# Three edits to a one-core spectral-filter and mixture-of-experts kernel: when lists are cast, in which order the last units run, which maxima are re-read first

## The chip, the cores and the metric

The kernel runs on one core of a Trainium2 chip. The metric is the device time of one execution in microseconds (us); lower is better. Engine names are those of the profile: PE is TensorE (PEld its weight loads), DVE is VectorE, ACT is ScalarE, POOL is GpSimd, SP is SyncE, which here only issues DMAs.

## The reference

```python
X = np.fft.rfft(x, axis=1)                       # x: 8 batches x 2496 rows x 256
y = np.fft.irfft(X * (filt_r + 1j*filt_i)[None], n=2496, axis=1)
x = y.reshape(8*2496, 256)
noisy = x @ w_gate + np.log1p(np.exp(x @ w_noise)) * noise      # 8 experts
top2 = two largest of each row; top2_w = softmax over those two
for each expert e:                                # w1[e]: 256x1024, w2[e]: 1024x256
    out[rows that chose e] += top2_w * (np.maximum(x[rows] @ w1[e], 0) @ w2[e])
```

## The kernel before, in words

**Two streams.** `fft_stream` filters the eight batches (the transform is written as matmuls), writes the filtered rows with their gate weights to a DRAM tensor `y`, and routes each batch: per expert, a list of row numbers in the DRAM tensor `lst`, and a small table `tabi` that says which stretch of which expert's list is the s-th block. `expert` works through blocks of rows that share an expert. `run` interleaves the two by a pace table; a scheduler of the framework then orders each engine's instructions by its own estimate, so that an edit in one place moves instructions nearly everywhere behind it.

**A block.** `read_list` issues, on SP, the load of a block's row numbers into the tile `lt` (line 1100), and POOL casts them to integers, `ids` (line 1106). `gather` fetches 128 rows at a time from `y` by an indirect DMA that POOL issues (line 1156) into slots of one staging tile `stage` (four slots for gathered rows, named "xg", handed out in turn by `slot`). `flip` lets SP transpose them by DMA, `turn` splits them into a high and a low part (`mxh`, `mxl`), and `expert` multiplies: `hps` is the first layer in PSUM, ACT and DVE turn it into `hh` and `hl` (lines 1369, 1370), `yps` is the second layer, ACT scales it by the gate into one of four output slots of `stage` (line 1396), and POOL issues an indirect DMA that adds the slot's rows to `out` (line 1397). These scatters to `out` wait for each other from unit to unit, because two experts may hold the same row; those of one unit do not.

**Order of the blocks.** First the blocks that can be taken after each batch, in `parts`; after the last batch seven single blocks of 512 rows (`SINGLE`), then what is left of each expert's list in units: 14 of 256 rows, then 4 of 128 rows (`ENDS`; the table's other slots are taken only in a branch at the end that these inputs do not enter). In each phase but `SINGLE`, the list of the next block is read, and cast, before the present block is handed on. A unit of either size loads both weight matrices of its expert, in two 16-bit planes each, by `load_planes`.

**Maxima.** From the fifth batch on the expert layers run on scaled 16-bit pairs. The scales come from maxima: `ymax` of the filtered rows, by `xscale`, and `wmax` of the weights, by `wscales`, a generator that is stepped now and then. `wscales` first loads all 64 quarter matrices of weights (line 595, 256 KB each) and lets ACT square them and sum each row (line 599). From each half of the sums `powers` makes a power of two on DVE and PE, kept in `wtab`. Then `wscales` re-reads the filtered rows of the first two batches from `y` in 12 loads (line 610) and lets DVE take their maxima (line 615), since those batches' own pass takes none. What is still left of it is run through at once when the first scaled block is gathered. POOL copies the scale of a block's expert from `wtab` to `sc` (line 1147); `w1h` and `w1l` (lines 1201, 1202) need `sc`, and `mxh` and `mxl` need `xs`, the result of `xscale`.

Of the kernel before, what the change touches and what calls it, by code (L numbers as in the profile page):

```python
# [14 lines left out]
I32 = mybir.dt.int32  # L15
# [13 lines left out]
E, F = 8, 1024  # L29
# [22 lines left out]
ENDS = (UNIT, USUAL, NUNIT), (UNIT // 2, E // 2, E)  # L52
SW = 32
# [97 lines left out]
class Moe:  # L151
# [427 lines left out]
    def xscale(self, bt):  # L579

        nc = self.nc
        nc.vector.tensor_reduce(self.xm, self.ymax[:, :2 * bt + 2], axis=AX.XY, op=ALU.max)
        q = yield from self.powers(self.xm, 1, TX)
        t = self.xs[bt + 1] = self.cp.tile([128, 2], F32, name=f"xs{bt}")
        nc.vector.tensor_copy(t, q[:, :, 0])
        yield

    def wscales(self):
# [50 lines left out]

        yield from pairs(load, top, 8 * E)  # L640
# [8 lines left out]
        yield from pairs(load_y, top_y, len(Y))  # L649
# [441 lines left out]
    def read_list(self, i, s, size):  # L1091
# [13 lines left out]
        ids = self.P.tile([128, n, nt], I32, name="ids", bufs=6)  # L1105
        nc.gpsimd.tensor_copy(ids, t)
        return ids, n, nt, s, self.tabs[i]
# [28 lines left out]
    def gather(self, blk, i):  # L1136
# [12 lines left out]
        if self.tail(tabi):  # L1149
            w = self.wodd = (self.wodd + 1) % 3  # L1150
            if nt < BLK // 128:
                w = self.load_planes(tabi, s, w)
        xg = []
# [252 lines left out]
    def run(self):  # L1406
# [15 lines left out]
        def parts():  # L1422

            def cut(blk, ready):
                for i in range(blk[1]):
                    yield (*blk, ready), i

            for i in range(NB):
# [5 lines left out]
                it = (self.read_list(i, s, m * BLK) for s in range(a, b))  # L1434

                nxt = next(it)
                while nxt is not None:
                    blk, nxt = nxt, next(it, None)
                    for p in cut(blk, i + 1):
                        state["left"] -= 1  # L1440
                        yield p
            state["left"] = 1
            for s in range(SINGLE):
                yield from cut(self.read_list(NB, s, BLK), NB)
            self.more = [self.nc.values_load(self.tabs[NB + 1 + i][0:1, 0, n:n + 1], min_val=0, max_val=E * CAPB * BLK // u)  # L1445
                         for i, (u, n, _) in enumerate(ENDS)]
            it = (self.read_list(NB + 1 + i, s, u) for i, (u, n, _) in enumerate(ENDS) for s in range(n))
            soon = [next(it)]
            while soon:
                soon += [b for b in (next(it, None),) if b]  # L1450
                yield from cut(soon.pop(0), NB)
# [69 lines left out]
```

## Time and profile before

| what | value |
|---|---|
| median of 3 runs | 2194.17 us (2190.20 to 2196.07) |
| profiled execution, its own time | 2191.23 us |
| its span, first to last instruction | 2189.4 us |
| busy: PE, PEld | 2107.5 us (96%), 1596.5 us (73%) |
| busy: DVE, ACT, POOL | 1473.3 us (67%), 1286.4 us (59%), 1024.6 us (47%) |
| granted PE clock over the span | 0.99 of full speed |

The profile is of one execution. Its own time lies 1.8 us above its span and 2.9 us below the median of the runs, within their spread. PE is busy nearly all the time, so a change can save only where PE is idle or its clock is not fully granted.

### The profile page before, as it was taken

To read this page: it belongs to the slowest core of one execution; us is meant where nothing else is said; L and a number is where in the kernel's file an instruction comes from. 1 tells how busy PE (TensorE), PEld (TensorE's weight loads), DVE (VectorE), ACT (ScalarE), POOL (GpSimd) and SP (SyncE) were. 2 spreads that over 40 slices of the span, in tenths; PEclk is the share of its full clock that TensorE was granted. 3 is DMA by queue.
4 is the path that set the end of the run, shared out by engine and by line. 5 is a ranking of instruction groups with operands and counts; after the bars stand their busy time and mean duration, and the time that the engine had idled before them with its cause. 6 is when DMAs were issued, how large, how long until landed. Compare 5 with 4: busy or idle time off the path is not lost. (4 is left out here: it accounts for less than half of the span.)

```text
span 2189.4 us, 42880 instructions
## 1 busy us (share of the span) xinstructions
PE 2107.5 (96%) x14517; PEld 1596.5 (73%) x14517; DVE 1473.3 (67%) x3245; ACT 1286.4 (59%) x2505; POOL 1024.6 (47%) x946
## 2 busy tenths in 40 slices
PE   8779999999999999899999999999999999999996
PEld 6437888888888888666666666766666666667886
DVE  4866678767986787778766886579666664333443
ACT  6666774777567746665665556555566564333443
POOL 4133424533443343545544453544566555654653
PEclk9989999999999999999999999999999999999999
DMA  9688987999888866967766666856899999768996
GB/s 241 173 247 203 230 222 171 222 234 228 203 213 230 189 144 152 202 160 174 156 155 151 136 146 149 198 118 131 198 246 238 230 238 211 200 148 221 277 273 170
DMA packets 511675, 428.49 MB, mean 196 GB/s; under 512 B 215680, under 2 KB 397016, under 8 KB 511448
## 3 DMA queue, kind: packets, MB, share of 16 engines
q1 hardware_dynamic: 450135, 341.27, 59.2%
q0 software_dynamic: 61312, 84.40, 22.5%
q8 instruction: 116, 1.90, 0.4%
q14 instruction: 112, 0.91, 0.1%
HBM read 263.92 MB, written 122.03 MB: 176 GB/s over the span
## 5 line engine op out<-in xcount | busy, mean ns | idle before, releaser
L1397 POOL DMA_INDIRECT out<-stage,ids x316 | 527.3, 1669 | 339.8 <-ACT stage L1396 245.9
L1370 DVE SCALAR_TENSOR_TENSOR hl<-hps,hh 128x512 f16<-128x512 f32 (+3 forms) x712 | 432.2, 624 | 339.5 <-ACT hh L1369 279.1
L1156 POOL DMA_INDIRECT stage<-y,ids x316 | 348.4, 1103 | 538.2 <-DMA xt<-stage 425.5
L124 PE MATMUL yps<-w,hh 128*128 128x256 f16 (+1 forms) x2048 | 558.8, 279 | 9.0 <-ACT hh L1369 3.8
L125 PE MATMUL yps<-w,hh 128*128 128x256 f16 (+1 forms) x2048 | 553.2, 277 | 0.0
L126 PE MATMUL yps<-w,hl 128*128 128x256 f16 (+1 forms) x2048 | 543.4, 278 | 6.8 <-DVE hl L1370 6.5
L1369 ACT ACTIVATE hh<-hps 128x512 f16<-128x512 f32 (+3 forms) x712 | 375.6, 550 | 185.7 <-PE hps L126 161.6
L125 PE MATMUL hps<-mxl,w1h 128*128 128x512 f16 (+1 forms) x1024 | 394.3, 386 | 0.7 <-DVE mxl L1244 0.7
L126 PE MATMUL hps<-mxh,w1l 128*128 128x512 f16 (+1 forms) x1024 | 393.0, 385 | 0.0
L124 PE MATMUL hps<-mxh,w1h 128*128 128x512 f16 (+1 forms) x1024 | 385.5, 388 | 2.7 <-DVE hl L1370 1.7
L1396 ACT ACTIVATE stage<-yps,gt 128x256 f32<-128x256 f32 x316 | 143.2, 475 | 342.3 <-PE yps L126 169.8
L124 PEld LDWEIGHTS <-hh 128*128 128x128 f16 x1760 | 172.3, 98 | 51.3 <-ACT hh L1369 4.1
L126 PEld LDWEIGHTS <-hl 128*128 128x128 f16 x1760 | 171.5, 98 | 48.9 <-issue 3.0
L125 PEld LDWEIGHTS <-hh 128*128 128x128 f16 x1760 | 172.2, 98 | 38.1 <-issue 6.0
L126 PEld LDWEIGHTS yps<-w,hl 128*128 128x128 f32 x768 | 145.9, 192 | 15.8 <-DVE hl L1370 8.2
L124 PEld LDWEIGHTS yps<-w,hh 128*128 128x128 f32 x768 | 147.0, 192 | 12.5 <-ACT hh L1369 4.9
L125 PEld LDWEIGHTS yps<-w,hh 128*128 128x128 f32 x768 | 146.6, 192 | 4.4 <-issue 0.6
L542 ACT COPY yt<-q 117x1024 uint16<-117x1024 uint16 x96 | 90.8, 946 | 42.4 <-PE q L536 23.6
L126 PEld LDWEIGHTS <-w1l 128*128 128x128 f16 x640 | 62.6, 98 | 71.8 <-issue 1.1
L1226 DVE COPY stage<-xt 128x1024 uint16<-128x1024 uint16 (+2 forms) x174 | 109.8, 685 | 3.0 <-issue 1.9
L125 PEld LDWEIGHTS <-w1h 128*128 128x128 f16 x640 | 62.6, 98 | 54.0 <-issue 4.0
L124 PEld LDWEIGHTS <-w1h 128*128 128x128 f16 x640 | 62.6, 98 | 53.0 <-issue 6.2
(287 smaller groups left out, 4041.7 us busy)
## 6 DMA issues: line engine op xcount, KB each, us to landing
stage<-w SPq DMA_DIRECT2D x328, 256.0 KB
x<-x SPq DMA_DIRECT2D x88, 256.0 KB
fd<-c SPq DMA_DIRECT2D x77, 240.0 KB
fi<-wpl SPq DMA_DIRECT2D x18, 1024.0 KB
fx<-fd SPq DMA_DIRECT2D x140, 128.0 KB
out<-z SPq DMA_DIRECT2D x24, 702.0 KB
wp<-w SPq DMA_DIRECT2D x64, 256.0 KB
fr<-w SPq DMA_DIRECT2D x16, 1024.0 KB
```

The lines of the kernel that those rows point to most:

```text
L124: nc.tensor.matmul(o, lh, rh, start=start, stop=False)
L125: nc.tensor.matmul(o, lh, rl, start=False, stop=False)
L126: nc.tensor.matmul(o, ll, rh, start=False, stop=stop)
L542: e = nc.scalar.copy(yt.bitcast(U16)[:, :k, :256].rearrange("p g (two d) -> p g two d", two=2), p.bitcast(U16)[:RP, :2 * m].rearrange("p ( ...
L1156: self.pin(lambda: nc.gpsimd.indirect_dma_start(out=x.bitcast(I32), out_offset=None, in_=self.y[:BLK + ready * ROWS], in_offset=bass.Indir ...
L1226: nc.vector.tensor_copy(xu.rearrange("p (t two) -> p two t", two=2), ent[3][0][:, 2 * kc:2 * kc + 2, :w])
L1369: hold(lambda: nc.scalar.activation(h, p, AF.Relu))
L1370: v = hold(lambda: nc.vector.scalar_tensor_tensor(l, p, 0.0, hf[0], op0=ALU.max, op1=ALU.subtract))
L1396: nc.scalar.activation(o, p, AF.Copy, scale=gate[:, t])
L1397: a = nc.gpsimd.indirect_dma_start(out=self.io["out"][:BLK + ready * ROWS], out_offset=bass.IndirectOffsetOnAxis(ap=ids[:, t:t + 1], axis= ...
```

## The change

Three edits. (1) `read_list` can return the cast as a function: the list's load is issued where it was, and POOL's cast is issued when the block begins. `SINGLE` and the units read one and two lists ahead. (2) The 4 units of 128 rows stand among the 14 of 256 (`MIXED`: after the 5th, 8th, 11th and 14th of them), so that the last two units are one of 256 and one of 128; `gather` skips slots until a unit's first slot is a multiple of its size. (3) `wscales` re-reads the filtered rows of the first batches before the weights instead of after them; `xscale` asserts that this is done.

```diff
+MIXED = sorted(((i, s) for i, (_, n, _) in enumerate(ENDS) for s in range(n)), key=lambda u: u[1] * 3 + 4 if u[0] else u[1])
...
     def xscale(self, bt):
...
+        assert self.seen
...
     def wscales(self):
...
+        yield from pairs(load_y, top_y, len(Y))
+        self.seen = True
         yield from pairs(load, top, 8 * E)
         for a, t in enumerate((TW1, TW2)):
             q = yield from self.powers(self.wmax[:, a * E:a * E + E], E, t, True)
...
-        yield from pairs(load_y, top_y, len(Y))
         self.scaled = True
...
-    def read_list(self, i, s, size):
+    def read_list(self, i, s, size, late=False):
...
-        ids = self.P.tile([128, n, nt], I32, name="ids", bufs=6)
-        nc.gpsimd.tensor_copy(ids, t)
-        return ids, n, nt, s, self.tabs[i]
+
+        def cast():
+            ids = self.P.tile([128, n, nt], I32, name="ids", bufs=6)
+            nc.gpsimd.tensor_copy(ids, t)
+            return ids, n, nt, s, self.tabs[i]
+
+        return cast if late else cast()
...
     def gather(self, blk, i):
...
+        while (self.turns.get("xg", -1) + 1) % nt:
+            self.slot("xg")
...
     def run(self):
...
-                it = (self.read_list(i, s, m * BLK) for s in range(a, b))
+                it = (self.read_list(i, s, m * BLK, True) for s in range(a, b))
...
-                    for p in cut(blk, i + 1):
+                    for p in cut(blk(), i + 1):
...
-            for s in range(SINGLE):
-                yield from cut(self.read_list(NB, s, BLK), NB)
-            self.more = [...]
-            it = (self.read_list(NB + 1 + i, s, u) for i, (u, n, _) in enumerate(ENDS) for s in range(n))
+            it = (self.read_list(NB, s, BLK, True) for s in range(SINGLE))
             soon = [next(it)]
             while soon:
                 soon += [b for b in (next(it, None),) if b]
-                yield from cut(soon.pop(0), NB)
+                yield from cut(soon.pop(0)(), NB)
+            self.more = [...]
+            it = (self.read_list(NB + 1 + i, s, ENDS[i][0], True) for i, s in MIXED)
+            soon = [next(it), next(it)]
+            while soon:
+                soon += [b for b in (next(it, None),) if b]
+                yield from cut(soon.pop(0)(), NB)
```

How the instructions stand now, at three places. Lines of the changed kernel are 1 to 9 above those of before (L617 is L615, L560 is L559, L577 is L576, L1406 is L1397).

DVE, where `wscales` begins, in the second batch's first blocks, before:

```order
L398 TENSOR_TENSOR tl<-fx,th 128x512
L340 TENSOR_TENSOR xl<-x,xh 117x512
L1079 TENSOR_TENSOR ro<-ro,rx 56x128
L1244 TENSOR_TENSOR mxl_2214<-xps,mxh_2213 128x512
L340 TENSOR_TENSOR xl<-x,xh 117x512
L426 TENSOR_TENSOR a<-q_1865,fr 128x512
```

And with the change:

```order
L341 TENSOR_TENSOR xl<-x,xh 117x512
L1082 TENSOR_TENSOR ro<-ro,rx 56x128
L1253 TENSOR_TENSOR mxl_2213<-xps,mxh_2212 128x512
L617 TENSOR_REDUCE ymax<-wp 117x1
L341 TENSOR_TENSOR xl<-x,xh 117x512
L427 TENSOR_TENSOR a<-q_1865,fr 128x512
L428 TENSOR_TENSOR b<-b,fi 128x512
L399 TENSOR_TENSOR tl<-fx,th 128x512
L617 TENSOR_REDUCE ymax<-wp 117x1
```

The 12 maxima of the re-read rows (`ymax<-wp`) moved here, among the next 95 rows of DVE.

PE, ahead of the first scaled block (`xm` is what `powers` transposes and multiplies, `pd` its powers of two), before:

```order
L126 MATMUL yps<-w_11225,hl 128x256
L446 MATMUL q_10083<-cf,a 128x2x64 x4
L576 MATMUL xm<-pd,small 128x1 x2
L457 MATMUL u_11105<-G,wg 32x360 x4
L343 MATMUL q_11129<-xh,hl 120x512
L344 MATMUL q_11129<-xh,hl 120x512
L345 MATMUL q_11129<-xl,hl 120x512
```

And with the change:

```order
L125 MATMUL yps<-w_11223,hh 128x256
L577 MATMUL xm<-pd,small 128x8 x2
L560 MATMUL xm<-ident,wmax 8x128
L126 MATMUL yps<-w_11223,hh 128x256
L127 MATMUL yps<-w_11223,hl 128x256
L577 MATMUL xm<-pd,small 128x8
L458 MATMUL u_11103<-G,wg 32x360 x4
L344 MATMUL q_11127<-xh,hl 120x512
L345 MATMUL q_11127<-xh,hl 120x512
L346 MATMUL q_11127<-xl,hl 120x512
L577 MATMUL xm<-pd,small 128x8
```

Before, only the scale of the filtered rows (`128x1`) stood this late; now both scales of the weights (`128x8`) do, the second with two matmuls between its transpose and its product.

POOL, the end of the units, before (numbers tell the units' lists apart):

```order
L1397 DMA out<-stage_84,ids_28198 21104x256
L1178 ISA
L1178 COPY gt_28958<-stage_84 128x1
L1180 TENSOR_SCALAR gt_28958<-gt_28958,sc_28942,xs7_20026 128x1
L1397 DMA out<-stage_84,ids_28392 21104x256
L1397 DMA out<-stage_84,ids_28584 21104x256
L1397 DMA out<-stage_84,ids_28778 21104x256
```

And with the change:

```order
L1187 ISA
L1187 COPY gt_28906<-stage_84 128x1
L1189 TENSOR_SCALAR gt_28906<-gt_28906,sc_28890,xs7_20024 128x1
L1406 DMA out<-stage_84,ids_28537 21104x256 x2
L1406 DMA out<-stage_84,ids_28696 21104x256 x2
L1406 DMA out<-stage_84,ids_28879 21104x256
```

Four scatters of four units, each behind the one before, ended the kernel; now the last are two of a unit of 256 rows, which need not wait for each other, and one of 128.

## Rows read from the trace of the kernel before

**Rows 1.** Busy time by stretch: us, engines (instructions), PEclk, DMA share, GB/s.

```profile
0.00:187.00 187.00, 153.60 (x817) 98.77 (x818) 123.54 (x383) 119.05 (x212) 52.23 (x54) 0.94 0.76 215
187.00:870.00 683.00, 666.64 (x4294) 583.02 (x4293) 521.77 (x1138) 461.28 (x932) 282.30 (x230) 1.00 0.86 204
870.00:905.00 35.00, 27.11 (x171) 20.51 (x169) 26.62 (x45) 18.36 (x35) 20.40 (x20) 0.95 1.11 206
905.00:1540.00 635.00, 630.57 (x4419) 431.86 (x4418) 475.63 (x1073) 377.83 (x692) 307.65 (x277) 1.00 0.69 154
1540.00:2175.00 635.00, 629.63 (x4824) 462.34 (x4822) 325.78 (x609) 309.93 (x636) 358.91 (x365) 1.00 0.93 226
2175.00:2189.40 14.40, 0.00 (x0) 0.00 (x0) 0.00 (x0) 0.00 (x0) 3.12 (x2) 0.62 0.18 22
```

**Rows 2.** Waits of PE, 830 to 905 us: total us, times, longest.

```profile
PE yps L126 <- DVE hl L1370: 4.2, 2, 3.4
PE q L446 <- DVE a L428: 1.3, 1, 1.3
PE u L457 <- ACT G L447: 0.8, 1, 0.8
```

**Rows 3.** Timeline of DVE, 868 to 898 us: start, us, instruction [idle before <-releaser].

```profile
875.36 0.95 DVE L615 TENSOR_REDUCE ymax<-wp 117x1 f32<-117x768 bf16 x1 [1.86 <-DMA wp<-y]
...
896.50 0.15 DVE L585 COPY xs<-xm 128x2 f32<-128x2 f32 x1
```

**Rows 4.** Lines 615 and 599: duration ns min/median/max, first and last start, forms.

```profile
L615 DVE TENSOR_REDUCE ymax<-wp x12: 929/1204/1221, 839.2 to 890.0; 117x1 f32<-117x1024 bf16 x8, 117x1 f32<-117x768 bf16 x4
...
L599 ACT ACTIVATE wp<-wp x64: 621/632/708, 187.4 to 734.8; 128x512 f32<-128x512 f32 x64
```

**Rows 5.** Timeline of POOL, the last scatters.

```profile
2169.94 1.59 POOL L1397 DMA_INDIRECT out<-stage,ids  x1 [6.30 <-ACT hh L1369]
2175.61 1.56 POOL L1397 DMA_INDIRECT out<-stage,ids  x1 [4.08 <-ACTq L1474]
2180.16 1.56 POOL L1397 DMA_INDIRECT out<-stage,ids  x1 [2.99 <-DMA out<-stage,ids]
```

**Rows 6.** Timeline of ACT, the last two outputs of units.

```profile
2168.68 0.47 ACT L1396 ACTIVATE stage<-yps,gt 128x256 f32<-128x256 f32 x1 [0.85 <-issue]
...
2174.12 0.47 ACT L1396 ACTIVATE stage<-yps,gt 128x256 f32<-128x256 f32 x1 [0.86 <-PE yps L126]
```

**Rows 7.** Waits of PE, 2145 to 2175 us.

```profile
PE yps L124 <- ACT hh L1369: 0.8, 3, 0.3
```

**Rows 8.** Timeline of PE, 1831 to 1834 us.

```profile
1833.71 0.27 PE L124 MATMUL yps<-w,hh 128*128 128x256 f16 x1 [1.66 <-ACT stage L1396]
```

**Rows 9.** Timeline of POOL, ahead of it.

```profile
1815.85 0.18 POOL L1106 CAST ids<-lt 128x4 int32<-128x4 f32 x1 [7.89 <-DMA lt<-lst]
...
1829.44 1.57 POOL L1397 DMA_INDIRECT out<-stage,ids  x1 [0.30 <-issue]
```

**Rows 10.** Waits of POOL over the span.

```profile
POOL ids L1106 <- DMA lt<-lst: 138.5, 32, 16.8
```

**Rows 11.** Busy time by stretch, as rows 1.

```profile
187.00:245.00 58.00, 53.23 (x323) 43.70 (x322) 34.78 (x59) 41.49 (x87) 28.65 (x27) 1.00 0.95 222
245.00:275.00 30.00, 30.00 (x193) 26.90 (x192) 21.92 (x36) 22.93 (x46) 11.25 (x10) 1.00 1.06 239
```

**Rows 12.** DMA queue of SP, 187 to 260 us: packets, MB, share of 16 engines.

```profile
q1 hardware_dynamic: 17047, 13.64, 71.9%
```

**Rows 13.** The same, 832 to 892 us.

```profile
q1 hardware_dynamic: 19337, 8.71, 65.2%
```

**Rows 14.** Timeline of DVE, small steps of `powers`, 757 to 761 us.

```profile
759.62 0.14 DVE L565 TENSOR_SCALAR pe<-pe 8x1 int32<-8x1 int32 x1
759.79 0.14 DVE L566 TENSOR_SCALAR pe<-pe 8x1 int32<-8x1 int32 x1
```

**Rows 15.** Timeline of ACT, first scaled weights.

```profile
863.88 0.72 ACT L1201 ACTIVATE w1h<-stage,sc 128x512 f16<-128x512 f32 x1 [2.44 <-DMA stage<-w]
```

More of the change, by code (lines that the diff above doesn't have):

```diff
@@ L1442, in parts @@
             state["left"] = 1
-            for s in range(SINGLE):
-                yield from cut(self.read_list(NB, s, BLK), NB)
-            self.more = [self.nc.values_load(self.tabs[NB + 1 + i][0:1, 0, n:n + 1], min_val=0, max_val=E * CAPB * BLK // u)
-                         for i, (u, n, _) in enumerate(ENDS)]
-            it = (self.read_list(NB + 1 + i, s, u) for i, (u, n, _) in enumerate(ENDS) for s in range(n))
+            it = (self.read_list(NB, s, BLK, True) for s in range(SINGLE))
             soon = [next(it)]
@@ L1450, in parts @@
                 soon += [b for b in (next(it, None),) if b]
-                yield from cut(soon.pop(0), NB)
+                yield from cut(soon.pop(0)(), NB)
+            self.more = [self.nc.values_load(self.tabs[NB + 1 + i][0:1, 0, n:n + 1], min_val=0, max_val=E * CAPB * BLK // u)
+                         for i, (u, n, _) in enumerate(ENDS)]
+            it = (self.read_list(NB + 1 + i, s, ENDS[i][0], True) for i, s in MIXED)
[3 more added lines that the diff above has]
+                yield from cut(soon.pop(0)(), NB)
         def may():
```

## The prediction

> **What bounds the kernel now.** I read the busy time by stretch first [rows 1]. The reader is to see that PE is the bound and where it is not: its idle time is 33.4 us up to 187 us (where the engines' order is not touched by the change), 16.4 from there to 870, 7.9 in the 35 us from 870 to 905, 4.4 to 1540, 5.4 to 2175, and 14.4 behind its last matmul. The change takes no matmul of a block away and adds none, so it can win at most these 48.5 us without the start, and only piece by piece. I then looked up who ends PE's waits at the places that the three edits touch: the waits and the timelines of 870 to 905 [rows 2, 3], of the last units [rows 5 to 7], of 1833 [rows 8, 9], and of 187 to 275, where DVE gets new work [rows 11].
>
> **The last units.** After the last output of ACT at 2174.12 [rows 6] POOL's last scatter starts only at 2180.16 [rows 5], 6.04 us later. The scatters form a chain: each starts 5.67 and then 4.55 us after the one before [rows 5], and the outputs come every 5.44 us [rows 6], so the chain was late already and the lateness is paid at the end. With the change the scatter before the last belongs to a unit of 256 rows. After its second output PE has 30 matmuls of 128 columns and 24 of 256 to do, against 48 and 24 for a unit of 128 now; a narrow one counting half, that is 39/48 of 5.44 = 4.4 us from its output to the last. Its scatter can start some 1.1 us behind the output's start (an estimate: 0.47 us for the output [rows 6] and as long again for the issue), that is 3.3 us ahead of the last output, and the last one 4.55 to 5.67 us behind it, 1.2 to 2.4 us behind the last output. Against 6.04 this wins 3.7 to 4.8 us; I take 4.3. What follows the last scatter is unchanged. Within the units of 128 PE waits 0.8 us in total for `hh` [rows 7]; among units of 256 their first layer stands beside 24 matmuls of the other unit. I take those 0.8 as won (0 to 0.8).
>
> **The casts.** POOL waits 138.5 us for lists [rows 10], but most of this lies beside PE's work: nobody waits for POOL as long as gathers are ahead and output slots are free. One place is visible: a cast that waits 7.89 us at 1815.85, four gathers and four scatters behind it that end at 1831 [rows 9], then ACT without a free output slot and PE idle for 1.66 us [rows 8]. With lists read a block earlier the cast finds its list there. I take 1.7 us (0 to 1.7). What the casts hid behind is POOL's own idle time; an earlier cast moves no DMA of the critical units except the list's own load, which I cost at nothing beside PE's 630 busy us of 635 [rows 1].
>
> **The maxima, at their old place.** From 870 to 905 PE idles 7.9 us, and the granted clock is 0.95 [rows 1]: after the longest wait (3.4 us [rows 2]) the matmuls run at the lower of the two levels for a while. 5% of 35 us are 1.75 us of lost clock, part of it in the idle time; I count 1.0. 4.2 us are waits for `hl` of DVE, 1.3 for `a` of DVE [rows 2]. DVE stood behind the re-read maxima: it waits 1.86 us for one load alone and gets `xs` ready only at 896.50 [rows 3], because the small steps of `powers` stand between maxima of about 1.2 us each [rows 4]. All this leaves. In its place come ACT's last squares of weights and the two scales of the weights, of which nothing was on the path before. Their price: ahead of the second product stand 12 small DVE steps, one every 0.17 us [rows 14], 2.0 us, with two matmuls (0.24 us) to cover them, 1.7 us; then the scale goes over POOL to ACT's first `w1h` of 0.72 us [rows 15], about 1.7 us against 1.6 us of other matmuls that stand in the order there, 0.1; and the third matmul of the block waits some 0.3 for `w1l`. Sum 2.1 us. The waits that have other causes (0.8 for `G` [rows 2], and 1.2 us of smaller ones) stay: 4.1 us in all, against 7.9 + 1.0. I take a gain of 4.8 us. The bounds are +8.9 (everything hidden) and -5 (the steps stand behind other DVE work, as the chain to `xs` did).
>
> **The maxima, at their new place.** The 12 reductions cost DVE 8 times 1.21 and 4 times 0.94, 13.4 us [rows 4], and they now stand in 187 to 275, where DVE is idle for 88 - 56.7 = 31.3 us and PE for 4.8 [rows 11]. ACT loses 12 squares of 0.63 us there. If DVE's idle time takes them, they cost nothing; if none is hidden, 13.4 us. DVE would go from 64% to 80% busy, and late `hl` shows on PE at once, so not nothing: I take 2 us, nearer to the free end because twice the needed time is idle.
>
> **The rest of the order.** From 187 to 1540 the scheduler places nearly every instruction anew. PE idles 16.4 + 4.4 us there [rows 1]; a new order can win or lose some of it. I take 0, and 6 us either way for the range.
>
> Sum: -4.3 - 0.8 - 1.7 - 4.8 + 2.0 = -9.6 us from the profiled execution's own 2191.23, that is 2181.6. The median of the runs is 2.9 us above that execution, so I forecast 2184.5 us, 0.44% under the median. A difference under 0.3% (6.6 us) cannot be told from none.
>
> **Rivals.**
> *The scales of the weights take the place of the maxima.* Both products and the copy to `sc` are now the last thing ahead of the first scaled block; if DVE or ACT is late there, PE waits as long as before. For it: the chain to `xs` took from 870 to 896.50 although its steps add up to 2 us. Against it: it was so slow because of the maxima that leave. Then only the other terms stay: 2191.2 - 6.8 + 2.0 + 2.9 = 2189.3, not to be told from before.
> *DVE becomes the bound early.* Place: 187 to 275. Each reduction waits for a load from DRAM, and DVE runs in order, so `hl` of the running block stands behind it. It decides as soon as loads are late as at 875 [rows 3]. Price: the full 13.4 us instead of 2, and the gain at 870 halved by ACT's squares there: 2184.5 + 11.4 + 2.4 = 2198.3, slower by 0.2%, and with the 6 us of the new order 2204, slower by 0.5%.
> *Small packets in the busiest stretch.* The re-read moves 10,296 packets of 256 bytes (12 loads, 117 partitions, 88 pieces in all for each of them) to where the DMA share is 0.95 to 1.06 [rows 11]. SP's queue takes 0.652 x 16 x 60 us / 19,337 = 32 ns a packet where the re-read stands now [rows 13] and 49 ns among the weights [rows 12]. At 32 ns the re-read takes 20.9 us of all 16 engines; the 12 loads of weights that it displaces, 3.1 MB at 239 GB/s [rows 11], 13.2 us. If the difference of 7.7 us came out at PE: 2192.2, no difference. The Trainium skill (DMA: Bandwidth & Descriptors, Specifications) says that transfers under 512 bytes miss line rate because the engine reads, modifies and writes; by that these loads should not go where the queues are fullest. The rows neither show nor exclude that mechanism: small packets take less time each than large ones, but more for their bytes.
> *The order happens to win* some of the 16.4 us up to 870: 2178.
>
> **How the numbers follow.** Forecast 0.50; weights' scales 0.27; early DVE 0.12; packets 0.06; lucky order 0.05. Faster by over 0.3%: 0.50 + 0.05, less 0.04 because the forecast ends 3 us from the bound and the new order can take that, plus 0.02 from the rivals' low side: 0.53. Slower: 0.12 of early DVE, of which some stays within 0.3%, and as much from the other rivals' high side: 0.13. The rest, 0.34, is no difference. The likeliest case's own range is 2177 to 2192. The range for all reaches up to early DVE's 2198 and down to a lucky order with the larger bound at 870: 2175 to 2198.
>
> **What would show each step.** Right: the start of the last scatter less that of the last output of ACT falls from 6.04 to 1 to 2.5 us; POOL's wait for lists falls to a tenth; no wait of 1.7 us for an output slot in the single blocks; the 12 maxima stand between 187 and 280 us with PE idle there at most 7 us; around the first scaled block PE idles about 4 us instead of 7.9 and the granted clock there is 1.0. Wrong: PE waits for `xm`, `w1h` or `mxh` of over 5 us there; DVE waiting for `wp<-y` early with `hl` late behind it; PE idle in 187 to 1540 above 30 us.

## The result: 1% slower, and the profile after

The changed kernel takes 2216.32 us (median of 4 runs, 2210.78 to 2224.62) against 2195.12 us of the kernel before (4 runs): ratio 1.0100, 95% interval 1.0060 to 1.0139. The forecast was 2184.5 with a range of 2175 to 2198, so it missed on the other side. The profiled execution took 2210.78 us with a span of 2209.0, that is 19.6 more than the span of before.

Busy time by stretch of the changed kernel, columns as in [rows 1]:

```profile
0.00:187.00 187.00, 153.48 (x818) 97.82 (x819) 123.24 (x383) 118.98 (x213) 51.93 (x54) 0.94 0.77 214
187.00:870.00 683.00, 655.72 (x4213) 572.42 (x4213) 523.25 (x1110) 449.77 (x908) 274.12 (x225) 0.99 0.85 202
870.00:905.00 35.00, 30.57 (x194) 27.42 (x192) 18.90 (x54) 17.94 (x39) 16.30 (x15) 0.95 0.78 182
905.00:1540.00 635.00, 625.74 (x4317) 425.76 (x4318) 463.81 (x1010) 373.99 (x682) 298.39 (x275) 0.98 0.68 153
1540.00:2175.00 635.00, 629.16 (x4740) 455.72 (x4739) 337.81 (x662) 315.16 (x635) 361.24 (x371) 1.00 0.93 228
2175.00:2209.00 34.00, 24.20 (x244) 21.61 (x242) 9.99 (x29) 11.18 (x31) 10.86 (x9) 0.90 0.36 72
```

Read it beside [rows 1]: PE works 10.9 us less from 187 to 870, 3.5 us more in the next 35, 4.8 us less from 905 to 1540. The 4.4 us that it idles from 870 to 905 look like the 4.1 of the prediction, but only because the first scaled block no longer falls into those 35 us, as shown below. Stretches of fixed time don't say how far the work has come, so a second reading is used below, **PE at equal work**: the matmuls are taken in order of time, each counts with the usual interval of its shape (the 25th percentile of before), and two profiles are compared at the times at which they reach the same sum. By it the changed kernel is 2.5 us late where the kernel before stands at 520 us, 12.7 at 732, 13.1 at 837, 17.9 at 899, 18.2 at 1158, 22.9 at 1520, 23.3 at 1976 and 25.2 at the last matmul; what follows that matmul is 5.6 us shorter. Some 70% is lost before 930 us, where the instructions stand in the same order as with the third edit alone.

**Near the first scaled block** the wait moved. Waits of PE, 870 to 930 us, of the changed kernel:

```profile
PE yps L125 <- ACT stage L1405: 2.3, 1, 2.3
PE hps L125 <- ACT w1h L1210: 2.3, 1, 2.3
PE xm L577 <- DVE pq L570: 1.7, 1, 1.7
```

Timelines of DVE, POOL, ACT and PE there:

```profile
895.12 1.38 DVE L1235 COPY stage<-xt 128x1024 uint16<-128x1024 uint16 x2 [4.55 <-DMA xt<-stage]
896.38 0.15 DVE L587 COPY xs<-xm 128x2 f32<-128x2 f32 x1
...
909.53 0.15 DVE L651 TENSOR_TENSOR wtab<-wtab,xm 128x8 f32<-128x8 f32 x1
...
911.65 1.62 POOL L1406 DMA_INDIRECT out<-stage,ids  x1 [0.30 <-issue]
914.38 0.19 POOL L1187 COPY gt<-stage 128x4 f32 x1 [1.10 <-DMA stage<-y,ids]
914.51 0.43 POOL L1154 COPY sc<-wtab 128x3 f32 x3
...
914.72 1.95 ACT L1210 ACTIVATE w1h<-stage,sc 128x512 f16<-128x512 f32 x3 [5.12 <-POOL sc L1154]
...
915.50 0.61 PE L125 MATMUL hps<-mxh,w1h 128*128 128x512 f16 x1 [2.32 <-ACT w1h L1210]
```

Two things are to be seen. The scale `xs` comes at 896.38, as late as before (896.50 in [rows 3]), although no maximum is left here: it stands on DVE behind the copy of the block's transposed rows, which waited 4.55 us. And the scales of the weights are ready at 909.53 (before at 827.6). On the way there DVE waits 3.66 and 3.87 us for the two small products of `powers`, which stand on PE among other matmuls; the copy to `sc` then stands on POOL for 5 us behind two DMA issues and a gate that waits for its rows. Before, the first scaled matmul ran at 898.60; now at 915.50. The rows of the kernel before for this are:

```profile
827.58 0.15 DVE L647 TENSOR_TENSOR wtab<-wtab,xm 128x8 f32<-128x8 f32 x1
...
893.91 1.37 DVE L1226 COPY stage<-xt 128x1024 uint16<-128x1024 uint16 x2 [0.77 <-DMA xt<-stage]
...
898.60 0.59 PE L124 MATMUL hps<-mxh,w1h 128*128 128x512 f16 x2
```

There too the copy of the transposed rows waited for its DMA, with no maximum left ahead of it. The granted clock of the changed kernel is 0.56 from 912 to 920, close to the lower of its two levels (1.2 GHz).

Where the maxima and the squares stand now (lines 617 and 601 are 615 and 599 in [rows 4]):

```profile
L617 DVE TENSOR_REDUCE ymax<-wp x12: 953/1210/1221, 187.9 to 279.4; 117x1 f32<-117x1024 bf16 x8, 117x1 f32<-117x768 bf16 x4
...
L601 ACT ACTIVATE wp<-wp x64: 617/632/677, 300.2 to 884.7; 128x512 f32<-128x512 f32 x64
```

**Between 300 and 870 us** one pattern is seen at most of PE's longer waits: within the 6 us ahead of 10 of the 13 of over 0.5 us, ACT runs squares of weights. ACT and then PE at 463:

```profile
463.69 0.63 ACT L601 ACTIVATE wp<-wp 128x512 f32<-128x512 f32 x1 [1.18 <-DMA wp<-w]
...
465.09 0.46 ACT L1405 ACTIVATE stage<-yps,gt 128x256 f32<-128x256 f32 x1
...
465.60 0.58 PE L125 MATMUL yps<-w,hh 128*128 128x256 f32 x1 [2.71 <-ACT stage L1405]
465.98 0.42 PE L126 MATMUL yps<-w,hh 128*128 128x256 f32 x1
466.19 0.41 PE L127 MATMUL yps<-w,hl 128*128 128x256 f32 x1
```

A square of weights waits for its load, a second one follows, the output that frees the bank of PE stands behind both, and PE idles 2.71 us; the matmuls after it come every 0.21 us instead of 0.12 (granted clock 0.68 from 466 to 470). Squares waited for loads in the kernel before too; which output stands behind them is decided by the order.

**The end** went as forecast in this profile. ACT's last two outputs and POOL's last two scatters:

```profile
2195.00 0.47 ACT L1405 ACTIVATE stage<-yps,gt 128x256 f32<-128x256 f32 x1 [1.41 <-PE yps L127]
2199.34 0.47 ACT L1405 ACTIVATE stage<-yps,gt 128x256 f32<-128x256 f32 x1 [0.86 <-PE yps L127]
...
2195.75 1.57 POOL L1406 DMA_INDIRECT out<-stage,ids  x1 [1.78 <-ACT stage L1405]
2200.39 1.56 POOL L1406 DMA_INDIRECT out<-stage,ids  x1 [3.08 <-ACT stage L1405]
```

The last scatter starts 1.05 us behind the last output, 6.04 before [rows 5, 6]. Waits of POOL over the span, for [rows 10]:

```profile
POOL ids L1111 <- DMA lt<-lst: 117.5, 25, 16.6
POOL ids L1111 <- DMA out<-stage,ids: 25.3, 10, 4.8
```

### The profile page after: what moved, and what is told of

It is laid out like the page before. It is cut to its first block, busy times and chain, and to the rows that moved or that the text cites. A ratio compares the mean times of both kernels' runs of the same rounds, so it can differ in the third digit from the quotient of the medians.

```text
span 2209.0 us, 42850 instructions
## 1 busy us (share of the span) xinstructions
PE 2118.9 (96%) x14517; PEld 1600.7 (72%) x14517; DVE 1477.0 (67%) x3245; ACT 1287.0 (58%) x2505; POOL 1012.9 (46%) x946
## 4 chain that ended last, share of the span: by engine, by line
PE 63%; DMA 4%; issue 2%; ACT 2%; DVE 2%; SPq 1%; POOL 0%; POOLq 0%; ACTq 0%; DVEq 0%
PE yps L127 9%; PE hps L125 9%; PE yps L125 9%; PE hps L126 9%; PE yps L126 9%; PE hps L127 9%; PE q L447 1%; DMA wp<-w 1%; PE q L511 1%; DMA stage<-y,ids 1%; DVE hl L1379 1%; PE q L535 1%; PE u L458 1%; ACT hh L1378 0%; DMA fx<-fd 0%
## 5 line engine op out<-in xcount | busy, mean ns | idle before, releaser
L1406 POOL DMA_INDIRECT out<-stage,ids x316 | 524.7, 1661 | 366.6 <-ACT stage L1405 284.1
L125 PEld LDWEIGHTS yps<-w,hh 128*128 128x128 f32 x768 | 147.6, 193 | 19.6 <-ACT stage L1405 10.2
```

What stands on the lines that cost most here:

```text
L125: nc.tensor.matmul(o, lh, rh, start=start, stop=False)
L1406: a = nc.gpsimd.indirect_dma_start(out=self.io["out"][:BLK + ready * ROWS], out_offset=bass.IndirectOffsetOnAxis(ap=ids[:, t:t + 1], axis= ...
```

## The experiments

All ratios are against runs of the kernel before on the same chip (its median differed from chip to chip). On two chips, those of "Each edit alone" and of `zip`, `shift15`, `shift1` and `step3`, the kernel before takes 2180 us; on the others 2192 to 2197. Profiles differ with the chip too: from 951 to 1970 us, PE's gaps add up to 0.5 to 2.1 us in the eight profiles of those two chips and to 5.4 to 11.2 us in the eleven others, the changed kernel and the one before among them. In the expectations, "gaps" are PE's idle pieces of over 0.4 us beyond the usual interval of each shape. Behind each ratio stands what it says of the expectation.

### Each edit alone

`max_only`: the kernel before with the third edit alone.

```diff
+        yield from pairs(load_y, top_y, len(Y))
         yield from pairs(load, top, 8 * E)
...
-        yield from pairs(load_y, top_y, len(Y))
         self.scaled = True
```

> The kernel before with the third edit alone: the maxima of the re-read rows ahead of the weights' squares. Theory A (the moved maxima cost it all: the squares of weights now run into the scaled blocks, stand ahead of ACT's outputs while they wait for their loads, and both weight scales end late): 16 to 22 us slower than before, with PE at equal work some 12 us late by 870 us and 17 us late by 930. Theory B (the late casts and the mixed units cost it, POOL being late for the output slots): within 6 us of before. Theory C (any new order of the instructions costs a few us by chance): 0 to 10 us slower, with no wait on PE behind a square of weights.

Measured: 2202.13 us, ratio 1.0091 (1.0069 to 1.0113): some 20 us slower, as theory A has it.

`max_back`: the changed kernel with these two lines back in their old places, so the first two edits alone.

> The changed kernel with the re-read maxima back behind the weights' scales, so late casts and mixed units alone. Theory A: 3 to 7 us faster than before (the end of the scatters gives some 5 us, the casts at most 1.7). Theory B: 10 us or more slower than before. Theory C: as theory A up to the units, since the order of PE, ACT and DVE is that of before until there, then up to 3 us worse.

Measured: 2178.80 us, ratio 0.9995 (0.9982 to 1.0008): no different from before. That is not theory B, and of theory A's 3 to 7 us at most 4 are left by the interval.

`late_only`: the first edit alone (`MIXED` and the alignment of slots taken out of `max_back`).

> The kernel before with the first edit alone: casts when the block begins. The order of PE, ACT and DVE is that of before. Theory A: 0 to 2 us faster (the wait of 1.7 us of PE for an output slot near 1833 us leaves). Theory B: 5 to 20 us slower, with PE waiting for output slots at several places. If casts late in the units wait for a free buffer of row numbers behind old scatters, that shows as casts ended by scatters, at no cost on PE.

Measured: 2181.28 us, ratio 1.0004 (0.9990 to 1.0019). No gap of PE of over 0.4 us is left after 1540 us; but none is left in `shift15` and `shift1` below either, which keep the old casts.

`mixed_only`: the second edit alone.

> The kernel before with the second edit alone: the 4 units of 128 rows among those of 256. Theory A: 3 to 6 us faster, the last scatter starting 1 to 2 us behind ACT's last output instead of 6.04, and up to 2 us lost to output slots at the units of 128 rows. Theory B: no change or slower, the units of 128 rows in the middle costing more than the end gives.

Measured: 2186.24 us, ratio 1.0022 (1.0008 to 1.0036): some 5 us slower, as theory B has it.

The third edit costs all of it: 1.0091 times 0.9995 is 1.0086, inside the interval of the whole change. Busy time by stretch of `late_only`, in which PE, ACT and DVE have the order of before, and below it of `max_only`:

```profile
187.00:870.00 683.00, 666.93 (x4300) 584.74 (x4299) 523.83 (x1137) 461.85 (x932) 276.73 (x230) 0.99 0.88 204
870.00:930.00 60.00, 52.60 (x318) 38.12 (x317) 44.60 (x74) 35.74 (x64) 28.60 (x30) 0.91 0.93 196
```

```profile
187.00:870.00 683.00, 656.27 (x4195) 573.01 (x4194) 522.00 (x1107) 447.89 (x902) 273.01 (x223) 0.99 0.85 201
870.00:930.00 60.00, 51.81 (x301) 38.78 (x300) 32.99 (x81) 34.52 (x73) 26.84 (x31) 0.89 0.74 182
```

PE at equal work, `max_only` is 3.6 us behind `late_only` at 406 us, 10.8 at 624, 17.9 at 835, 19.1 at 951, and still 19.1 at 1968: nothing is lost or won behind the first scaled block. Four profiles with the order of before there (before, `late_only`, `max_back`, `mixed_only`) have PE busy for 666.3 to 668.6 us from 187 to 870, so 10 us there are no scatter of one execution.

At the end the second edit alone does harm. The last casts, outputs and scatters of `mixed_only`:

```profile
2144.30 0.19 POOL L1107 CAST ids<-lt 128x1 int32<-128x1 f32 x1 [6.28 <-DMA lt<-lst]
...
2178.71 1.55 POOL L1400 DMA_INDIRECT out<-stage,ids  x1 [3.83 <-DMA out<-stage,ids]
...
2170.11 0.47 ACT L1399 ACTIVATE stage<-yps,gt 128x256 f32<-128x256 f32 x1 [0.86 <-PE yps L127]
```

A list that is not there yet holds POOL for 6.28 us, the chain of scatters is late again, and its last link starts 8.60 us behind the last output. In `max_back`, with casts late and lists read earlier, it starts 2.54 us behind it (5.53 in `max_only`, which has the old end, on the same chip):

```profile
2162.73 0.47 ACT L1403 ACTIVATE stage<-yps,gt 128x256 f32<-128x256 f32 x1 [0.86 <-PE yps L127]
...
2165.27 1.55 POOL L1404 DMA_INDIRECT out<-stage,ids  x1 [3.30 <-issue]
```

### What in the third edit costs: squares later, maxima early, or only another order?

Theory A1 is that the squares, 15 steps later, cost; A2 that the early maxima do; C that any new order costs by chance.

`zip`: the changed kernel, re-reads in the same steps as the first weights, so that squares stand where they stood.

```diff
-        yield from pairs(load_y, top_y, len(Y))
-        self.seen = True
-        yield from pairs(load, top, 8 * E)
+        ys = pairs(load_y, top_y, len(Y))
+        for _ in pairs(load, top, 8 * E):
+            next(ys, None)
+            yield
+        self.seen = True
```

> The changed kernel with the 12 re-reads taken in the same steps as the first weights instead of in 15 steps of their own ahead of them, so that the maxima are early and the squares of weights stand where they stood before the change. Theory A1 (the shift of the squares by 15 steps costs it, the early maxima themselves little): 1 to 8 us faster than before, PE at equal work within 4 us of the kernel with late casts alone by 870 us, and the scales of the weights ready before 800 us, so no wait on them near the first scaled block. Theory A2 (the maxima on DVE and their small packets in the fullest stretch cost it): 10 to 20 us slower than before, like the changed kernel. Theory C (any new order costs by chance): 0 to 10 us slower.

Measured: 2204.17 us, ratio 1.0098 (1.0076 to 1.0121): some 21 us slower, like the changed kernel. A1 alone is wrong.

`shift15`, `shift1`, `shift5`, `shift3`: the kernel before with so many empty steps ahead of the squares.

```diff
+        for _ in range(15):
+            yield
         yield from pairs(load, top, 8 * E)
```

> The kernel before with 15 empty steps ahead of the squares of weights, nothing else moved: the squares stand where the third edit puts them, the maxima stay behind the scales. Theory A1: PE at equal work 8 to 16 us later than in the kernel with late casts alone by 830 us, and a further loss near the first scaled block, where squares, scales and all maxima meet; 15 to 35 us slower than before in all. Theory A2: within 4 us by 830 us, a loss only near the first scaled block.

Measured: 2187.08 us, ratio 1.0037 (1.0020 to 1.0054): some 8 us slower, about half of the least that A1 said. Its squares run from 294.6 to 855.1 us, those of `max_only` from 300.2 to 888.2, on chips with the same time before. PE at equal work is 5.4 us behind `late_only` at 835 us here and 17.9 in `max_only`, so the larger part of that loss goes with the early re-reads and not with the later squares.

> The kernel before with one empty step ahead of the squares of weights, that is, the squares one step later. Theory A1 in the form that only a late end of the squares costs: within 3 us of before. Theory C (where each square falls among the filter's steps is chance, and any other place costs): 3 to 12 us slower, with PE waiting at other places between 300 and 750 us.

Measured: 2180.56 us, ratio 1.0000 (0.9986 to 1.0015): within A1's 3 us, not theory C's 3 to 12.

> The kernel before with 5 empty steps ahead of the squares of weights: another neutral new order. Theory C: PE's gaps of over 0.4 us from 187 to 870 us add up to 24 to 30 us instead of 17 to 19 with the order of before, as with 1 step (25.5) and 15 steps (27.9). If the order of before is not a good one among its like: 15 to 22 us.

Measured: 2197.96 us, ratio 1.0019 (1.0007 to 1.0030); gaps from 187 to 870 us of 25.3 us, as theory C has it.

> The kernel before with 3 empty steps ahead of the squares, one more neutral order. If the order of before is a good one among its like: PE busy 658 to 662 us from 187 to 870, gaps of over 0.4 us 24 to 29 us there. If the three others were chance: 664 us or more, gaps under 22.

Measured: 2188.34 us, ratio 0.9994 (0.9975 to 1.0014); gaps of 27.5 us and PE busy for 659.5, so the order of before is a good one among its like up to 870 us; the time is no different.

`step3` and `before_step3`: `STEP = 3` instead of 4, in the changed kernel and in the one before.

> The changed kernel with the generator of the scales stepped every third step of the filter instead of every fourth, so that squares and scales end earlier than the first scaled block. Theory A1: the 5 us lost from 870 to 930 come back, and part of what was lost between 450 and 750 too, though the squares then lie closer to each other: 4 to 14 us faster than the changed kernel, 6 to 16 us slower than before. Theory A2: no faster than the changed kernel by 870 us.

Measured: 2206.49 us, ratio 1.0122 (1.0100 to 1.0143): some 27 us slower than before, and no faster than the changed kernel.

> The kernel before with the generator of the scales stepped every third step: squares, scales and maxima all end before the first scaled block, in the old succession. If a new order alone costs 6 to 8 us and the gain of 4.8 us near the first scaled block is real: 0 to 5 us slower than before, with gaps from 870 to 930 us of 0 to 4 us. If denser squares cost more: 5 to 15 us slower.

Measured: 2209.59 us, ratio 1.0088 (1.0066 to 1.0110): some 19 us slower, more than either range; gaps from 870 to 930 of 14.6 us, so the forecast gain isn't there either.

`zip_dve` and `zip_dma`: the kernel before with half of `zip` added, the real re-reads staying late: 12 reductions of a resident table without loads, or 12 loads without reductions.

```diff
+        ys = pairs(lambda i: i, dull, len(Y))      # zip_dma: pairs(load_y, None, len(Y))
+        for _ in pairs(load, top, 8 * E):
+            next(ys, None)
+            yield
-        yield from pairs(load, top, 8 * E)
```

> The kernel before with 12 extra reductions of the re-reads' sizes on DVE, over a table that is always on the chip, in the same steps as the first weights; no load, result unused; the real maxima stay late. Theory A2 in the form that the work on DVE costs it: 10 to 15 us slower than before, PE at equal work 8 us or more late by 300 us. In the form that the loads and the waits for them cost it: within 4 us by 300 us. Theory C (any new order costs): 2 to 10 us slower, with the loss spread up to 870 us and at other places than in the changed kernel.

Measured: 2225.74 us, ratio 1.0133 (1.0091 to 1.0175): some 29 us slower, beyond all three ranges. PE at equal work is 6.5 us behind the kernel before at 300 us and 24 at 837, without any load.

> The kernel before with 12 extra loads of the filtered rows in the same steps as the first weights, into the buffers that the re-reads use, and no reduction of them; the real re-reads stay late. Loads cost it: 10 to 20 us slower than before, PE 8 us or more late by 300 us. The work on DVE or its waits cost it: within 4 us by 300 us. Theory C: 2 to 10 us slower, spread.

Measured: 2206.43 us, ratio 1.0068 (1.0046 to 1.0091): some 15 us slower, in the range of the loads, though PE at equal work is 5.4 us late at 300 us and not 8.

`aft_shift8`: the changed kernel with 8 empty steps ahead of the re-reads.

> The changed kernel with 8 empty steps ahead of the re-reads: the maxima are still early, the order a new one. If the early maxima themselves cost it: as slow as the changed kernel or slower, gaps of over 0.4 us from 187 to 870 us of 28 us or more. If the changed kernel's order was an unlucky one: 5 to 15 us faster than the changed kernel, gaps of 20 to 26 us.

Measured: 2211.33 us, ratio 1.0089 (1.0058 to 1.0120); gaps of 30.7 us from 187 to 870: the early maxima cost it in another order as well.

`spread` and `spread_late`: the changed kernel with a re-read in every fourth step of the weights, or in every third from the 21st on.

```diff
+        for k, _ in enumerate(pairs(load, top, 8 * E)):
+            if k % 4 == 0:
+                next(ys, None)
+            yield
```

> The changed kernel with one re-read in every fourth step of the weights, so that the 12 maxima are spread over most of the time of the squares, and the squares stand where they stood before. If crowding on DVE costs: PE busy 658 to 662 us from 187 to 870, as with empty steps, gaps 25 to 28 us, and 1 to 8 us slower than before. If early re-reads cost wherever they stand: PE busy 648 to 656 us, 15 us or more slower than before.

Measured: 2196.70 us, ratio 1.0019 (1.0004 to 1.0034): some 4 us slower, as if crowding on DVE costs (PE busy for 657.8 us and gaps of 28.9 lie just outside what was named). `zip` and `spread` differ only in how close the re-reads stand, one in every step or in every fourth; the squares start at the same place and the scales of the weights are ready at 848.7 and 840.6 us. 1.0098 against 1.0019 is the plainest sign that crowding costs.

> The changed kernel with the re-reads in every third step of the weights from the 21st on: squares where they stood before, the order of before up to some 450 us, maxima done before 760 us. If what the changed kernel lost was the crowding and the late scales of the weights: 0 to 6 us faster than before, and PE busy 660 us or more from 187 to 870. If the scale of the filtered rows is held by the copy of the transposed rows and not by the maxima: it comes at 890 us or later here too, PE's gaps from 870 to 930 us are 4 us or more, and the time is within 6 us of before.

Measured: 2202.87 us, ratio 1.0029 (1.0008 to 1.0050): no gain but some 6 us lost; the second case came, with `xs` at 893.0 us and gaps from 870 to 930 of 7.8 us.

`two`: `max_back` with two of the late maxima in each step.

> Late casts and mixed units as in the changed kernel, the maxima behind the weights' scales as before, but two of them in each step, so that they end earlier; the order is that of before up to some 760 us. If the maxima at the first scaled block were what held PE there, and if only a new order ahead of it cost time: 3 to 8 us faster than before, PE's gaps from 870 to 930 us 0 to 4 us instead of 7 to 9. If two maxima a step are still not done by then or if the scale's own chain holds PE: no different from before.

Measured: 2197.38 us, ratio 1.0024 (1.0009 to 1.0040); gaps from 870 to 930 of 14.3 us, with the maxima still at 835 to 878 us. Neither case came: it is some 5 us slower. `xs` comes at 895.5 us, when the last maximum is long done and DVE has waited 5.01 us for the transposed rows; what costs the 5 us was not followed up.

Busy time by stretch in turn of `shift3`, `zip_dve`, `zip_dma` and `spread`:

```profile
187.00:870.00 683.00, 659.45 (x4241) 577.74 (x4240) 521.31 (x1134) 456.81 (x926) 269.04 (x230) 0.99 0.87 204
870.00:930.00 60.00, 58.77 (x370) 44.15 (x369) 52.29 (x84) 42.65 (x77) 31.13 (x30) 1.00 0.93 210
```

```profile
187.00:870.00 683.00, 648.26 (x4144) 564.14 (x4144) 510.43 (x1107) 445.35 (x905) 271.83 (x221) 0.99 0.84 198
870.00:930.00 60.00, 49.32 (x298) 40.47 (x297) 40.71 (x79) 31.40 (x61) 27.65 (x28) 0.89 0.94 201
```

```profile
187.00:870.00 683.00, 659.06 (x4228) 576.72 (x4227) 517.35 (x1125) 454.26 (x917) 274.65 (x229) 0.99 0.87 204
870.00:930.00 60.00, 53.76 (x311) 40.06 (x310) 46.37 (x77) 36.70 (x68) 26.71 (x27) 0.91 0.99 214
```

```profile
187.00:870.00 683.00, 657.76 (x4203) 572.32 (x4202) 522.97 (x1134) 450.90 (x914) 279.47 (x228) 0.99 0.85 202
870.00:930.00 60.00, 56.95 (x363) 44.35 (x362) 40.62 (x72) 40.84 (x75) 31.02 (x29) 0.97 0.80 200
```

All four lose against the 666 to 669 us of the old order: `shift1`, `shift5`, `shift3` and `shift15` have 661.1, 660.8, 659.5 and 658.5 us. But the neutral orders get most of it back in the next 60 us (57.0 to 60.0 us busy against 51.2 to 53.8 of the old order). The table shows what goes with it, from the timelines: when ACT copied the last filtered rows (`yt`) ahead of the first `xs`, and when `xs` was copied.

| kernels | last `yt`, us | `xs`, us | ratio |
|---|---|---|---|
| old order (before, `late_only`, `max_back`, `mixed_only`) | 865.5 to 869.1 | 892.6 to 896.5 | 0.9995 to 1.0022 |
| neutral orders (`shift1`, 3, 5, 15) | 847.9 to 862.6 | 873.9 to 891.2 | 0.9994 to 1.0037 |
| `two`, `spread_late` | 871.5, 871.3 | 895.5, 893.0 | 1.0024, 1.0029 |
| early maxima (changed, `max_only`, `aft_shift8`, `spread`) | 877.8 to 880.3 | 894.5 to 900.4 | 1.0100, 1.0091, 1.0089, 1.0019 |
| `zip_dma`, `zip` | 879.0, 886.3 | 904.9, 905.6 | 1.0068, 1.0098 |
| `zip_dve` | 895.0 | 925.7 | 1.0133 |
| `before_step3`, `step3` | 896.1, 901.0 | 906.1, 913.1 | 1.0088, 1.0122 |

The first scaled block needs the fifth batch's filtered rows: they must be written, gathered, transposed and copied before its matmuls. In the neutral orders they come 7 to 21 us earlier than in the kernel before, so PE, late by then, merely waits less. With more work on the filter's engines and queues ahead of that time (the maxima, denser squares, loads) they come 9 to 32 us later.

Late rows are not all. `zip` has them 17 us later than the kernel before and still gets back 6.0 of the 24.6 us that PE at equal work is behind `late_only` at 835 us, by 951; its scales of the weights are ready at 848.7 us. `max_only`, with rows 11 us later and these scales ready at 912.0, loses another 1.2 us there, and the changed kernel, with 909.5, another 4.8 from 837 to 899 against the kernel before. `spread`, with its rows as late as those of `max_only` and the scales at 840.6, has PE busy for 56.95 instead of 51.81 us from 870 to 930. Each row of the table is of single executions: that of `spread` is the slowest of its ten (2205.61 us), those of `shift1` and `shift15` are the fastest of theirs, so part of how late or early their rows come is the execution's own.

The timeline of DVE in `spread_late`, where all maxima are done by 675 us and all scales of the weights by 834:

```profile
882.70 0.69 DVE L1382 SCALAR_TENSOR_TENSOR hl<-hps,hh 128x512 fp32r<-128x512 f32 x1
891.69 1.39 DVE L1238 COPY stage<-xt 128x1024 uint16<-128x1024 uint16 x2 [8.30 <-DMA xt<-stage]
892.98 0.14 DVE L587 COPY xs<-xm 128x2 f32<-128x2 f32 x1
```

And PE's longest wait there, 870 to 930 us:

```profile
PE q L344 <- DVE xs L587: 5.9, 1, 5.9
```

With both chains gone that were said to hold PE, DVE idles 8.30 us for the transposed rows, and a matmul of the filter waits 5.9 us until `xs` behind them is copied. The waits for `hl` did leave with the maxima, but of the 9.1 us of PE's gaps from 870 to 930 us in the kernel before, 7.8 are left. By this kernel, most of what the late maxima of the kernel before filled is a wait that is there anyway.

## Why the prediction was wrong

**The step that failed first: "All this leaves", a gain of 4.8 us from 870 to 905.** From [rows 2, 3] the waits for `hl` and `a` and the late `xs` were put down to the maxima ahead of them on DVE. The runs showed `xs` at 893 to 913 us with the maxima done long before. In `spread`, `spread_late` and `zip` it comes behind the copy of the transposed rows, for which DVE idles 7.0, 8.3 and 5.9 us; in both kernels with a step of 3 it comes ahead of that copy, 10 to 12 us behind the last filtered rows, which are themselves late. The maxima stood beside the wait for the rows. The chain of filter, gather and transposes was never costed.

**"In its place come ... 2.1 us"** was too small as well. That was the rival of the weights' scales, given 0.27 and priced at no loss against before. It came true at a higher price: the way over POOL, counted as 0.1 us beside other matmuls, took 5 us because the copy to `sc` stands behind a gather, a scatter and a gate on POOL, and DVE waited 7.5 us in all for the two products on PE. PE at equal work lost 4.8 us from 837 to 899.

**"The rest of the order ... I take 0, and 6 us either way" is where the size was lost.** PE idles 41.0 us from 187 to 1540, above the 30 named as a sign of being wrong. From 187 to 870 it lost 10.9 us of busy time. Four neutral orders lost 5.5 to 8.2 there against before, so a gain by chance was not to be expected with the same weight as a loss. They had it back at the first scaled block, to within 0.4% of the time. The changed kernel didn't. Two things go with that: its filtered rows came 8.7 us later than before, and its scales of the weights 82 us later; which of them weighs how much no run separates.

**"2 us, nearer to the free end"** for the 12 reductions at their new place was right for what shows up at once (from 187 to 280 us PE idles 5.5 us, 0.7 more than before; at equal work it is not behind by 400 us, `max_only` 3.6 us behind `late_only`) and wrong for what they set back. Crowded among the squares they are worth up to 18 us of PE's time by 870 (`zip`, 648.2 us busy; `zip_dve`, 648.3, without any load), 10 to 13 more than a neutral order, nearly the 13.4 us named as the bound. In the changed kernel the squares had made room for them, and it was 3 to 5 us more than neutral orders. The argument from idle time (31.3 us for 13.4) counted engines' shares. That the filter is a chain through DVE whose delay is paid when a block needs its last row, 600 us later, fits the late rows of `zip` and `zip_dve`; it is argued and not shown by itself.

**Small packets** were no rival of much weight by 870 us: `zip_dma` has 659.1 us busy there, as neutral orders, though at equal work it is 10 us behind the kernel before at 837 us, where these are 1 to 8. Its total, 0.68% slower, says that loads cost something, as its filtered rows come 10 us later; how much of that is the size of the packets isn't separated. From 187 to 260 us SP's queue took this in the changed kernel (columns as [rows 12]):

```profile
q1 hardware_dynamic: 22729, 13.18, 76.9%
```

That is 5,682 packets more and 7% more time (76.9 against 71.9% of the engines) for less data than before, 39.5 ns a packet instead of 49. The Trainium skill (DMA: Bandwidth & Descriptors, Specifications) says that transfers under 512 bytes miss line rate; bytes per time fell by 10% here, which agrees. The reason that it gives, a read-modify-write, no run here shows.

**The last units: right in this profile, in part by luck.** Forecast 1.2 to 2.4 us from the last output to the last scatter, measured 1.05; 5.0 us won for 4.3. Over the eight profiles with the first two edits it is 1.05 to 6.39 us: in `zip`, `spread` and `spread_late` (4.85, 5.61, 6.39) the scatters ahead of the last are late already and the lateness is paid at the end as before. The ten profiles with the old end have 2.96 to 6.04. What was missed is that the mixed order alone makes it worse (8.60 us), and that the units of 128 rows in the middle wait for output slots (PE at 2078 and 2154 us, 1.8 us in total), where 0.8 us of gain were forecast. Both edits together came to a ratio of 0.9995, not to be told from none; the 6.8 us forecast for them (4.3, 0.8 and 1.7) lie outside its interval, which ends at a gain of 4 us.

**The casts: not borne out.** The wait of 1.7 us for an output slot was gone in `late_only`, with no time to show for it (ratio 1.0004). But it is absent as well in `max_only`, `mixed_only`, `shift1` and `shift15`, which keep the old casts, on the two chips where the kernel before takes 2180 us; and `two`, with late casts on another chip, has one of 1.0 us. So no run shows that the edit removes it. POOL's wait for lists didn't fall to a tenth but from 138.5 to 117.5 us, and 25.3 us of waits came up for a free buffer of `ids`, held by older scatters.

**What stays open.** The changed kernel loses 4.7 us at equal work between 930 and 1540 us against before, though PE, ACT and DVE have there the order of `max_only`, which loses nothing against `late_only`. It goes with the chip, as far as the profiles tell: the kernel before, with the order of `late_only` on PE, ACT and DVE, falls 8 us behind it from 951 to 1968 us. What differs between the chips is open. That the filter's late rows are why early maxima aren't given back rests on what goes together in 19 profiles, with the late scales of the weights beside it; no run brought the rows forward by itself.

## What to carry to other kernels

Before an engine's late work is moved away from a wait, ask what else ends that wait: follow the waiting block's own data back (rows, gather, transposes, scale), and count on a gain only if that chain would have been ready earlier. Idle time on an engine is no room for new work if a chain runs through it whose end another stage needs; look at when that end is needed, not only at what the neighbours lose at once. Where a scheduler places everything anew, run a few neutral edits first: they tell what any new order costs here and where it is given back. And before an edit is credited with a wait that is gone, see whether the wait is there at all in the profile of a kernel without that edit on the same chip.

## What the runs showed of the hardware that was not expected

Of five waits of PE of 2.2 to 2.9 us from 187 to 870 us in the changed kernel, three were followed by the lower level of the clock and two were not. After 2.71 us idle ahead of 465.6 the granted clock was 0.68 from 466 to 470: 1.3 us of those 4 lost, with matmuls every 0.21 us at first and every 0.12 from 469 on. After 2.89 us ahead of 504.7 and 2.19 ahead of 686.0 it was 0.71 (504.7 to 508) and 0.62 (686 to 690). After 2.23 us ahead of 217.4 and 2.60 ahead of 305.9 it stayed at 1.00. So a wait of this length may cost half as much again, or nothing; the length alone doesn't tell.

Where such waits follow each other, at the first scaled block, the clock was 0.50 from 899 to 902, 1.00 from 902.1 to 905.4 and 0.50 again from 905.5 to 919. From 870 to 930 that makes 0.86, against 0.97 before and 0.91 to 0.94 in the three other profiles with the order of before.
